# A Mamba-2 scan with an ELU feed-forward behind it: blocks of two batches by turns, and the scan's products of two blocks in one go

## The chip, the cores and the metric

The kernel runs on one core of one Trainium2 chip. The metric is the device time of one execution in microseconds (us). The kernel before takes 390.7 us (median of its runs). Kernels are compared only within the same rounds.

## The reference

The first half is a chunked Mamba-2 scan for 4 batches, 8 heads, 768 tokens, head size 32 and state size 16. The second half is a feed-forward on all 3072 tokens (256 to 2048 to 256) with an ELU between. Everything is float32; the two weights come in as float64.

```python
for c in range(nc):                                   # chunks along the sequence
    cum = np.cumsum(log_a[:, :, sl], axis=-1)
    L = np.exp(cum[:, :, :, None] - cum[:, :, None, :]) * causal
    M = np.einsum('bhin,bhjn->bhij', Cc, Bc) * L      # "scores", then weighed
    y_intra = np.einsum('bhij,bhjd->bhid', M, xc)     # "inside"
    y_inter = np.einsum('bhin,bhnd->bhid', Cc, state) * np.exp(cum)[..., None]   # "across"
    y[:, :, sl] = y_intra + y_inter
    state = decay_full * state + sum_j(Bx)            # "sums", "states"
# bridge: (B,H,S,D) -> (B*S, H*D)
h = x @ w_in
g = np.where(h > 0.0, h, np.exp(np.minimum(h, 0.0)) - 1.0)
return g @ w_out
```

The output of a chunk needs the state that the chunk before it left, so blocks of one batch form a chain. Blocks of different batches do not depend on each other.

## The kernel before: the parts that matter here

The tokens are cut into 12 blocks of 256 (3 per batch). TensorE does the feed-forward of block n-2 (second product, `l2`) and of block n (first product, `l1`) by turns in steps of 8 passes, and between these steps it visits the scan of the next blocks. A visit consists of many small products on parts of the array. A float32 product shows in the trace as two passes (MATMUL records), each with a load of its weights (one more record; the trace of before has 3546 of each); counts of the scan's small products below are counts of such passes.

```python
def sums(n, pool=p_a, tag="a"):          # one block; 24 or 32 of its small products
    ...
            nc.tensor.matmul(
                out=ps[v][32 * q:32 * q + 32, u],
                lhsT=s["sc"][toks, u, 2 * q:2 * q + 2].rearrange("p h n -> p (h n)"),
                rhs=s["x"][toks, u, 2 * D * q:2 * D * (q + 1)], start=True, stop=True,
                tile_position=(Q * v, 32 * q), skip_group_check=True)

def meet(n):                             # one visit of one block
    across(n)
    inside(n)
    if n + 1 < NP:
        sums(n + 1)
        states(n + 1)

for n in range(2, NP):
    for i in range(8):
        l2(n - 2, i)                     # second product of block n-2, step i
        if todo < len(pieces):
            w_take(todo, nc.vector)      # ScalarE's Abs of a weight piece, ...
        l1(n, i)                         # first product of block n, step i
        if todo < len(pieces):
            w_give(todo)                 # ... VectorE and GpSimd finish the piece
            w_load(todo + 6)
            todo += 1
        while lag:
            elu()
        if i == 0:                       # transfers of the next blocks
            if n + 2 < NP:
                load_bc(n + 2)
                spread_cum(n + 2)        # the decay matrix L, right after B and C
                load_x(n + 2)
            if n + 3 < NP:
                spread_exp(n + 3)
        ...                              # (cut: block 3's own steps)
        if n + 2 < NP:
            if i == 1:
                scaled(n + 2, nc.gpsimd)
            if i == 3:
                turn(n + 2)
                turn_exp(n + 2)
            if 2 <= i < 6:
                decay(n + 2, i - 2)      # ScalarE's exponentials of L
        ...
        if i == 6 and n + 1 < NP:
            meet(n + 1)
        if i == 7 and n + 2 < NP:
            scores(n + 2)
            for q in range(4):
                weigh(n + 2, q)
```

The order of these lines is also the order in which each engine gets its instructions: in the profile after the change, ScalarE begins nothing of what stands behind one waiting instruction for 15.6 us. The float64 weights are turned into float32 on the chip while the first blocks run: `todo` counts the 16 pieces, and pieces 10 to 15 are still being made when n = 2 (one in each of its steps 0 to 5).

## Time and profile before

| | before |
|---|---|
| median of 6 runs in the first comparison | 390.7 us (390.14 to 393.05) |
| span of the profiled run, mean granted clock | 388.0 us, 1.000 |
| TensorE busy | 98% of the span |
| cost of one scan visit with its sums | 1.66 to 1.75 us |
| cost of one scores visit | 0.82 us |

The last two rows come from the starts of single products: the time from the feed-forward group in front of a visit to the end of the group behind it, less 16 feed-forward passes at 0.2157 us. The busy shares and the way a block's scan sits between the feed-forward groups are shown in the prediction. The line below gives the chain of waits that ended last, as shares of the span by engine.

```profile
PE 83%; ACT 5%; DMA 3%; SPq 3%; DVE 3%; issue 1%; POOL 0%; DVEq 0%; ACTq 0%; POOLq 0%
```

"issue" is time in which an engine waited for nothing that the profile shows. Here it is 1%.

### The profile page before, as it was taken

Reading aid. Unit: us, or ns where it says so; the run is one execution under the profiler, and the core shown is the slowest. Engines: PE = TensorE matmul, PEld = TensorE weight load, DVE = VectorE, ACT = ScalarE, POOL = GpSimd, SP = SyncE. Lnnn points to the kernel's source line nnn. Section 1 sums busy time; section 2 is a strip of 40 time slices with the busy share of each in tenths; the row PEclk is TensorE's granted clock in tenths of the full one; section 3 lists DMA queues with packets and bytes.
Section 4 is the critical chain, followed back from the end, with each engine's and each line's share of the span. In section 5 each row is a group of like instructions: output and inputs, shape, how many; then the busy total and the mean of one; then the engine's idle time right before and its main releaser. Section 6 shows DMA issues by size and latency. Waiting matters only on the chain.

```text
span 388.0 us, 8744 instructions
## 1 busy us (share of the span) xinstructions
PE 381.7 (98%) x3546; PEld 323.8 (83%) x3546; DVE 136.8 (35%) x280; ACT 200.1 (52%) x480; POOL 73.0 (19%) x133
## 2 busy tenths in 40 slices
PE   8999999999999999999999999999999999999996
PEld 4678788888888888888888888888888888888885
DVE  4877867943323232323123233223232321221000
ACT  3969879662653563563554464455366234334000
POOL 6525426540120120011021012012012000000000
DMA  8979966016007007006105303402500000000000
GB/s 165 225 165 256 280 157 119 7 37 113 4 12 133 7 3 137 14 2 123 28 0 88 65 0 53 101 0 45 95 2 29 2 0 11 20 2 27 0 29 27
DMA packets 86921, 25.02 MB, mean 64 GB/s; under 512 B 77184, under 2 KB 81504, under 8 KB 86880
## 3 DMA queue, kind: packets, MB, share of 16 engines
q1 hardware_dynamic: 84704, 24.26, 29.7%
q8 instruction: 28, 0.46, 0.5%
q10 hardware_dynamic: 2176, 0.20, 0.4%
q14 instruction: 13, 0.11, 0.1%
HBM read 21.10 MB, written 3.34 MB: 63 GB/s over the span
## 4 chain that ended last, share of the span: by engine, by line
PE 83%; ACT 5%; DMA 3%; SPq 3%; DVE 3%; issue 1%; POOL 0%; DVEq 0%; ACTq 0%; POOLq 0%
PE ps_o L552 38%; PE ps_h L525 36%; PE ps_o L567 4%; PE ps_y L497 2%; ACT L L393 2%; SPq L107 2%; PE ps_g L412 1%; DMA w<-in_moe_w_in_dram 1%; PE ps_y L482 1%; DMA xr<-in_x_dram 1%; ACT e L537 1%; DMA flat<-F 1%; PE ps_st L438 1%; ACT mag L152 1%; SPq L115 1%
## 5 line engine op out<-in xcount | busy, mean ns | idle before, releaser
L525 PE MATMUL ps_h<-yT,w_in 128*128 128x256 f32 x768 | 181.3, 380 | 1.1 <-DVE g L539 0.5
L552 PE MATMUL ps_o<-w_out,g 128*128 128x256 f32 x704 | 167.3, 382 | 0.1
L525 PEld LDWEIGHTS ps_h<-yT,w_in 128*128 128x128 f32 x768 | 145.5, 190 | 22.0 <-ACT yT L508 0.9
L552 PEld LDWEIGHTS ps_o<-w_out,g 128*128 128x128 f32 x704 | 131.7, 190 | 19.5 <-issue 1.4
L539 DVE SCALAR_TENSOR_TENSOR g<-e,ps_h 128x512 f32<-128x512 f32 x96 | 65.9, 687 | 209.7 <-ACT e L538 209.6
L537 ACT ACTIVATE e<-ps_h 128x512 f32<-128x512 f32 x96 | 57.1, 595 | 137.2 <-PE ps_h L525 137.0
L538 ACT ACTIVATE e<-e 128x512 f32<-128x512 f32 x96 | 60.5, 630 | 3.0
L398 POOL TENSOR_SCALAR_AFFINE_SELECT L<-L 64x512 f32<-64x512 f32 x40 | 26.6, 665 | 132.4 <-ACT L L393 131.2
L393 ACT ACTIVATE L<-L,ncum 128x64 f32<-128x64 f32 x160 | 41.9, 334 | 0.0
L508 ACT COPY yT<-ps_y 64x128 f32<-64x128 f32 (+1 forms) x70 | 17.9, 260 | 6.7 <-PE ps_y L497 5.7
L459 POOL TENSOR_TENSOR Sx<-S_new,hmask 128x64 f32<-128x64 f32 x44 | 13.3, 304 | 20.8 <-DVE S_new L454 14.1
L421 DVE TENSOR_TENSOR M<-ps_g,L 128x256 f32<-128x256 f32 x48 | 17.1, 416 | 0.1
L558 ACT COPY ob<-ps_o 128x512 f32<-128x512 f32 x11 | 6.4, 585 | 18.4 <-PE ps_o L552 18.4
L321 POOL TENSOR_TENSOR sc<-bc,eb 128x256 f32<-128x256 f32 x12 | 7.8, 656 | 38.9 <-DMA bc<-in_B_dram 37.2
L567 PE MATMUL ps_o<-w_out,g 128*128 128x256 f32 x64 | 14.0, 379 | 0.0
L567 PEld LDWEIGHTS ps_o<-w_out,g 128*128 128x128 f32 x64 | 12.2, 190 | 1.6
L194 POOL TENSOR_TENSOR w_out<-mag,w_out 128x512 uint32<-128x512 uint32 x8 | 10.2, 1274 | 16.5 <-DVE mag L184 16.5
L194 POOL TENSOR_TENSOR w_in<-mag,w_in 128x512 uint32<-128x512 uint32 x8 | 10.2, 1277 | 15.2 <-DVE mag L184 15.2
L184 DVE SCALAR_TENSOR_TENSOR mag<-mag,sgn 128x512 uint32<-128x512 uint32 x16 | 12.3, 772 | 0.5
L454 DVE SCALAR_TENSOR_TENSOR S_new<-S_new,ec,ps_st 128x64 f32<-128x64 f32 x40 | 11.2, 279 | 2.5
L152 ACT ACTIVATE mag<-w 128x512 f32<-128x512 f32 x16 | 10.7, 671 | 1.5 <-DMA w<-in_moe_w_in_dram 1.3
L497 PE MATMUL ps_y<-M,xr 64*32 64x64 f32 x768 | 10.6, 225 | 0.0
(67 smaller groups left out, 137.5 us busy)
## 6 DMA issues: line engine op xcount, KB each, us to landing
L<-flat SPq DMA_DIRECT2D x20, 256.0 KB, 4.5
w<-in_moe_w_in_dram SPq DMA_DIRECT2D x8, 512.0 KB, 5.0
w<-in_moe_w_out_dram SPq DMA_DIRECT2D x8, 512.0 KB, 6.4
xr<-in_x_dram SPq DMA_DIRECT2D x24, 128.0 KB, 4.4
out_dram<-ob SPq DMA_DIRECT2D x11, 256.0 KB, 2.2
bc<-in_B_dram SPq DMA_DIRECT2D x24, 64.0 KB, 3.2
bc<-in_C_dram SPq DMA_DIRECT2D x22, 64.0 KB, 3.4
ec<-flat_exp SPq DMA_DIRECT2D x64, 16.0 KB, 1.8
```

What stands on the lines that cost most here:

```text
L194: nc.gpsimd.tensor_tensor(out=w, in0=w_mag[i][:, :, cols], in1=w, op=ALU.add)
L393: nc.scalar.activation(L[:, h, u], L[:, h, u], ACT.Exp, bias=ncum[:, u, row:row + 1])
L398: nc.gpsimd.affine_select(out=part, in_=part, pattern=[[0, 4], [0, 2], [1, Q]], compare_op=ALU.is_ge, fill=0.0, base=0, channel_multiplier=-1)
L421: nc.vector.tensor_tensor(out=M, in0=s["g"][q], in1=s["L"][:, 2 * q:2 * q + 2].rearrange("p k u i -> p u k i"), op=ALU.mult)
L497: nc.tensor.matmul(out=s["y"][t][v][col:col + D, u], lhsT=s["x"][toks, u, D * h:D * (h + 1)], rhs=s["M"][h // 2][toks, u, h % 2], start=Fa ...
L508: nc.scalar.copy(out=yT[n][at:at + count, t, :, Q * v:Q * v + Q], in_=s["y"][t][v][src:src + count])
L525: nc.tensor.matmul(out=ps[:, j], lhsT=w_in[:, k, m * P:(m + 1) * P], rhs=yT[n][:, k].rearrange("p u i -> p (u i)"), start=(k == 0), stop=( ...
L537: nc.scalar.activation(e, ps, ACT.Relu, scale=-1.0)
L538: nc.scalar.activation(e, e, ACT.Exp, scale=-1.0)
L539: nc.vector.scalar_tensor_tensor(out=g_of[n][:, 2 * i:2 * i + 2], in0=e, scalar=1.0, in1=ps, op0=ALU.subtract, op1=ALU.max)
L552: nc.tensor.matmul(out=o_of[n][:, ts], lhsT=g_of[n][:, m, ts * P:(ts + 1) * P], rhs=w_out[:, m], start=(m == 0 and ts == 0), stop=(m == MC ...
L567: nc.tensor.matmul(out=ps, lhsT=g_of[n][:, m, ts * P:(ts + 1) * P], rhs=w_out[:, m], start=(m == 0), stop=(m == MC - 1))
```

## The change

The intent is to save changes of tile shape on TensorE (0.145 to 0.198 us each in the trace of before, against 0.018 between two groups of the same shape). If the blocks of two batches come by turns (batch 0, batch 1, batch 0, ...), blocks 2k and 2k+1 do not depend on each other, and their scores, across, inside and sums can be done in one visit. From block 4 on there are then four visits of each kind instead of eight. The transfers of both blocks of a pair are issued in one round, in a new order. Block 3's exponentials are brought by eight small transfers instead of one product.

```diff
+    def place(n):
+        return 2 * (n // (2 * NG)) + n % 2, n // 2 % NG
 ...
-    def scores(n):                    # likewise sums, across, inside
-        gs = [psum([P, 2, 2, Q], "ps_g") for _ in range(4)]
+    def scores(*ns):
+        gs = [psum([P, len(ns), 2, 2, Q], "ps_g") for _ in range(4)]
+        for at, n in enumerate(ns):
 ...
+    def meet(*ns):
+        inside(across(*ns), *ns)
+        then = ns[-1] + 1, ns[-1] + 2
+        if then[0] < NP:
+            sums(*then)
+            for n in then:
+                states(n)
 ... in the start:
             spread_cum(3)
             load_x(3)
+            spread_exp(3)             # was first_exp(3), a product on TensorE
 ... in the main loop:
-            if i == 0:
-                if n + 2 < NP:
-                    load_bc(n + 2)
-                    spread_cum(n + 2)
-                    load_x(n + 2)
-                if n + 3 < NP:
-                    spread_exp(n + 3)
+            late = 2 if n == 2 else 3
+            m = n + late
+            if m % 2 == 0 and 4 <= m < NP:
+                if i in (0, 1):
+                    load_bc(m + i)
+                    load_x(m + i)
+                    spread_exp(m + i)
+                if i in (2, 3):
+                    spread_cum(m + i - 2)
+                if i in (4, 5):
+                    scaled(m + i - 4, nc.gpsimd)
+            m = n + 2 - n % 2
+            if 4 <= m < NP:
+                if n % 2 == 0:
+                    ...
+                    if i >= 2:
+                        decay(m + i // 6, (i - 2) % 4)
+                else:
+                    ...
+                    if i == 3:
+                        scores(m, m + 1)
+                        for q in range(4):
+                            weigh(m, q)
+                            weigh(m + 1, q)
+                    if i == 6:
+                        meet(m, m + 1)
 ... (cut: rows_of and the outputs by place(n), buffer counts, one copy on GpSimd)
```

More of the change, by code (lines that the diff above doesn't have):

```diff
@@ L70 @@
     const = ctx.enter_context(tc.tile_pool(name="const", bufs=1))
-    raw = ctx.enter_context(tc.tile_pool(name="raw", bufs=4))
+    raw = ctx.enter_context(tc.tile_pool(name="raw", bufs=3))
     att = ctx.enter_context(tc.tile_pool(name="att", bufs=2))
@@ L95 @@
     st = {}
+    def place(n):
+        return 2 * (n // (2 * NG)) + n % 2, n // 2 % NG
     def rows_of(n):
-        b, g = divmod(n, NG)
+        b, g = place(n)
         return slice(BH * g + NH * b, BH * g + NH * (b + 1))
     def load_bc(n, c_queue=nc.sync):
-        b, g = divmod(n, NG)
+        b, g = place(n)
         st.setdefault(n, {})["bc"] = raw.tile([P, 2, 2, NH, N], F32, tag="bc", name="bc")
@@ L110, in load_x @@
     def load_x(n):
-        b, g = divmod(n, NG)
-        st[n]["x"] = raw.tile([P, 2, NH * D], F32, tag="xr", name="xr")
+        b, g = place(n)
+        st[n]["x"] = raw.tile([P, 2, NH * D], F32, tag="xr", name="xr", bufs=4)
         for u in range(2):
@@ L150, in w_abs @@
     def w_abs(i):
-        w_mag[i] = conv.tile([P, 2, CW], U32, tag="mag", name="mag", bufs=3)
+        w_mag[i] = conv.tile([P, 2, CW], U32, tag="mag", name="mag")
         nc.scalar.activation(w_mag[i].bitcast(F32), w_words(i)[1].bitcast(F32), ACT.Abs)
@@ L198 @@
     w_load(0)
-    idle = const.tile([P, 4, P], BF16, name="idle")
+    idle = att.tile([P, 4, P], BF16, tag="M", name="idle", bufs=8)
     nc.vector.memset(idle, 0.0)
@@ L242 @@
         out=minus, in0=ident, scalar1=-1.0, scalar2=None, op0=ALU.mult)
-    heads = [const.tile([ROWS, NH, N], F32, name=f"heads{n}") for n in range(4)]
-    for n in range(4):
+    heads = [const.tile([ROWS, NH, N], F32, name=f"heads{n}") for n in range(3)]
+    for n in range(3):
         nc.gpsimd.tensor_copy(
@@ L400, in decay @@
                     compare_op=ALU.is_ge, fill=0.0, base=0, channel_multiplier=-1)
-    def scores(n):
-        s = st[n]
-        s["g"] = gs = [psum([P, 2, 2, Q], "ps_g") for _ in range(4)]
-        for u in range(2):
-            for v in range(2):
-                for q in range(4):
-                    rows, toks = slice(32 * q, 32 * q + 32), slice(Q * v, Q * v + Q)
-                    nc.tensor.matmul(
-                        out=gs[q][toks, u], lhsT=s["bt"][rows, u, toks],
-                        rhs=s["ctm"][rows, u, :, toks], start=True, stop=True,
-                        tile_position=(32 * q, Q * v), skip_group_check=True)
-        s["M"] = []
+    def scores(*ns):
+        gs = [psum([P, len(ns), 2, 2, Q], "ps_g") for _ in range(4)]
+        for at, n in enumerate(ns):
+            s = st[n]
+            for u in range(2):
+                for v in range(2):
+                    for q in range(4):
+                        rows, toks = slice(32 * q, 32 * q + 32), slice(Q * v, Q * v + Q)
+                        nc.tensor.matmul(
+                            out=gs[q][toks, at, u], lhsT=s["bt"][rows, u, toks],
+                            rhs=s["ctm"][rows, u, :, toks], start=True, stop=True,
+                            tile_position=(32 * q, Q * v), skip_group_check=True)
+            s["g"], s["M"] = [g[:, at] for g in gs], []
     def weigh(n, q):
@@ L426, in chunks, with sums @@
     def chunks(n):
-        return [(u, v) for u in range(2) for v in range(2) if n % NG < NG - 1 or u + v < 2]
-    def sums(n, pool=p_a, tag="a"):
-        s = st[n]
-        s["st"] = ps = [psum([P, 2, 2 * D], "ps_st"),
-                        pool.tile([P, 2, 2 * D], F32, tag=tag, name="ps_st")]
-        for u, v in chunks(n):
-            toks = slice(Q * v, Q * v + Q)
-            for q in range(4):
-                nc.tensor.matmul(
-                    out=ps[v][32 * q:32 * q + 32, u],
-                    lhsT=s["sc"][toks, u, 2 * q:2 * q + 2].rearrange("p h n -> p (h n)"),
-                    rhs=s["x"][toks, u, 2 * D * q:2 * D * (q + 1)], start=True, stop=True,
-                    tile_position=(Q * v, 32 * q), skip_group_check=True)
+        return [(u, v) for u in range(2) for v in range(2)
+                if place(n)[1] < NG - 1 or u + v < 2]
+    def sums(*ns, pool=p_a, tag="a"):
+        ps = [psum([P, len(ns), 2, 2 * D], "ps_st"),
+              pool.tile([P, len(ns), 2, 2 * D], F32, tag=tag, name="ps_st")]
+        for at, n in enumerate(ns):
+            s = st[n]
+            for u, v in chunks(n):
+                toks = slice(Q * v, Q * v + Q)
+                for q in range(4):
+                    nc.tensor.matmul(
+                        out=ps[v][32 * q:32 * q + 32, at, u],
+                        lhsT=s["sc"][toks, u, 2 * q:2 * q + 2].rearrange("p h n -> p (h n)"),
+                        rhs=s["x"][toks, u, 2 * D * q:2 * D * (q + 1)], start=True, stop=True,
+                        tile_position=(Q * v, 32 * q), skip_group_check=True)
+            s["st"] = [p[:, at] for p in ps]
     def states(n):
-        b, g = divmod(n, NG)
+        b, g = place(n)
         s = st[n]
@@ L456, in states @@
                     in1=add, op0=ALU.mult, op1=ALU.add)
-            Sx = att.tile([P, 2, D], F32, tag="Sx", name="Sx", bufs=8)
+            Sx = att.tile([P, 2, D], F32, tag="Sx", name="Sx", bufs=12)
             nc.gpsimd.tensor_tensor(
@@ L462, in states, with across @@
             at = 2 * u + v + 1
-            starts[n + at // 4, at % 4 // 2, at % 2] = Sx
+            starts[n + at // 4 * 2, at % 4 // 2, at % 2] = Sx
     def shift(n, v):
         return 2 * D * v if n else 0
-    def across(n):
-        s = st[n]
-        s["y"] = y = [[psum([P, 2, Q], "ps_y") for _ in range(2)] for _ in range(2)]
+    def across(*ns):
+        y = [[psum([P, len(ns), 2, Q], "ps_y") for _ in range(2)] for _ in range(2)]
         for u in (1, 0):
-            for v in range(2):
-                Sx = starts.pop((n, u, v), None)
-                if Sx is None:
-                    continue
-                for q in range(4):
-                    rows, col = slice(32 * q, 32 * q + 32), (64 * q + shift(n, v)) % P
-                    nc.tensor.matmul(
-                        out=y[q // 2][v][col:col + 64, u],
-                        lhsT=Sx[rows].rearrange("p k d -> p (k d)"),
-                        rhs=s["cts"][rows, u, Q * v:Q * v + Q], start=(u == 1), stop=False,
-                        tile_position=(32 * q, col), skip_group_check=True)
@@ L488, in inside @@
-    def inside(n, ts=(0, 1)):
-        s = st[n]
-        for t in ts:
-            for u in range(2):
+            for at, n in enumerate(ns):
                 for v in range(2):
-                    toks = slice(Q * v, Q * v + Q)
+                    Sx = starts.pop((n, u, v), None)
+                    if Sx is None:
+                        continue
                     for q in range(4):
-                        h, col = 4 * t + q, (D * q + shift(n, v)) % P
+                        rows, col = slice(32 * q, 32 * q + 32), (64 * q + shift(n, v)) % P
@@ L497, in inside @@
                         nc.tensor.matmul(
-                            out=s["y"][t][v][col:col + D, u],
-                            lhsT=s["x"][toks, u, D * h:D * (h + 1)],
-                            rhs=s["M"][h // 2][toks, u, h % 2], start=False, stop=True,
-                            tile_position=(Q * v, col), skip_group_check=True)
-            if t == 0:
-                yT[n] = ffn.tile([P, KC, 2, P], F32, tag="yT", name="yT")
+                            out=y[q // 2][v][col:col + 64, at, u],
@@ new lines, in across, with inside @@
+                            lhsT=Sx[rows].rearrange("p k d -> p (k d)"),
+                            rhs=st[n]["cts"][rows, u, Q * v:Q * v + Q],
+                            start=(u == 1 and at == 0), stop=False,
+                            tile_position=(32 * q, col), skip_group_check=True)
+        return y
+    def inside(y, *ns):
+        for t in range(2):
+            for at, n in enumerate(ns):
+                s = st[n]
+                for u in range(2):
+                    for v in range(2):
+                        toks = slice(Q * v, Q * v + Q)
+                        for q in range(4):
+                            h, col = 4 * t + q, (D * q + shift(n, v)) % P
+                            nc.tensor.matmul(
+                                out=y[t][v][col:col + D, at, u],
+                                lhsT=s["x"][toks, u, D * h:D * (h + 1)],
+                                rhs=s["M"][h // 2][toks, u, h % 2], start=False, stop=True,
+                                tile_position=(Q * v, col), skip_group_check=True)
+            n = ns[0]
+            if n // 2 not in yT:
+                yT[n // 2] = ffn.tile([P, KC, 2, 2, P], F32, tag="yT", name="yT")
+            out = yT[n // 2][:, t, n % 2:n % 2 + len(ns)]
@@ L508, in inside @@
                     nc.scalar.copy(
-                        out=yT[n][at:at + count, t, :, Q * v:Q * v + Q],
-                        in_=s["y"][t][v][src:src + count])
-        if 1 in ts:
+                        out=out[at:at + count, :, :, Q * v:Q * v + Q],
+                        in_=y[t][v][src:src + count])
+        for n in ns:
             st.pop(n)
@@ L526, in l1 @@
                     out=ps[:, j], lhsT=w_in[:, k, m * P:(m + 1) * P],
-                    rhs=yT[n][:, k].rearrange("p u i -> p (u i)"),
+                    rhs=yT[n // 2][:, k, n % 2].rearrange("p u i -> p (u i)"),
                     start=(k == 0), stop=(k == KC - 1))
@@ L541, in elu, with row_of @@
             op0=ALU.subtract, op1=ALU.max)
+    def row_of(n):
+        b, g = place(n)
+        return b * S + g * BLK
     o_of = {}
@@ L558, in l2 @@
             nc.scalar.copy(out=ob, in_=o_of.pop(n))
+            r0 = row_of(n)
             nc.sync.dma_start(
-                out=out[n * BLK:(n + 1) * BLK, :].rearrange("(t p) e -> p t e", p=P), in_=ob)
+                out=out[r0:r0 + BLK, :].rearrange("(t p) e -> p t e", p=P), in_=ob)
     def l2_last(n):
@@ L571, in l2_last @@
             nc.scalar.copy(out=ob[:, ts], in_=ps)
-            r0 = n * BLK + ts * P
+            r0 = row_of(n) + ts * P
             nc.sync.dma_start(out=out[r0:r0 + P, :], in_=ob[:, ts])
-    def meet(n):
-        across(n)
-        inside(n)
-        if n + 1 < NP:
-            sums(n + 1)
-            states(n + 1)
+    def meet(*ns):
[5 more added lines that the diff above has]
+                states(n)
     def w_take(i, low):
@@ L619 @@
     turn_exp(0)
-    sums(0, p_o, "o")
+    sums(0, pool=p_o, tag="o")
     first_minus(*first)
@@ L634 @@
         weigh(0, q)
-    nc.gpsimd.tensor_copy(F[3 * BH:4 * BH, 0], F[BH:2 * BH, 0])
-    second = (1, 0, 1), (1, 1, 3)
+    second = (1, 0, 0), (1, 1, 3)
     first_low(1, 0)
@@ L641 @@
     w_low(1, nc.scalar)
-    across(0)
-    inside(0)
+    inside(across(0), 0)
     w_sign(1)
@@ L672 @@
     scores(1)
-    sums(1, p_o, "o")
+    sums(1, pool=p_o, tag="o")
     weigh(1, 0)
@@ L681 @@
     w_take(4, nc.vector)
-    across(1)
-    inside(1)
+    inside(across(1), 1)
     ncum = turned(F[0:ROWS, 0], "ncum", -1.0, nc.vector)
@@ L714 @@
             load_x(3)
+            spread_exp(3)
             weigh(2, 2)
             weigh(2, 3)
-            sums(2, p_o, "o")
+            sums(2, pool=p_o, tag="o")
             states(2)
         if s == 10:
-            across(2)
-            inside(2)
+            inside(across(2), 2)
         if len(lag) > 1:
             elu()
-    spread_exp(4)
     for n in range(2, NP):
@@ L751 @@
                     turn(3)
-                    first_exp(3)
                     turn_exp(3)
@@ L757 @@
                         weigh(3, q)
-            if n + 2 < NP:
-                if i == 1:
-                    scaled(n + 2, nc.gpsimd)
-                if i == 3:
-                    turn(n + 2)
-                    turn_exp(n + 2)
-                if 2 <= i < 6:
-                    decay(n + 2, i - 2)
-            if i == 4 and n == 2:
-                sums(3)
-                states(3)
-            if i == 6 and n + 1 < NP:
-                meet(n + 1)
-            if i == 7 and n + 2 < NP:
-                scores(n + 2)
-                for q in range(4):
-                    weigh(n + 2, q)
+                if i == 4:
+                    sums(3)
+                    states(3)
+            late = 2 if n == 2 else 3
[12 more added lines that the diff above has]
+                if n % 2 == 0:
+                    if i in (5, 7):
+                        turn(m + i // 7)
+                        turn_exp(m + i // 7)
+                    if i >= 2:
+                        decay(m + i // 6, (i - 2) % 4)
+                else:
+                    if i < 2:
+                        decay(m + 1, i + 2)
+                    if i == 3:
+                        scores(m, m + 1)
+                        for q in range(4):
+                            weigh(m, q)
+                            weigh(m + 1, q)
+                    if i == 6:
+                        meet(m, m + 1)
+            if n == 2 and i == 6:
+                meet(3)
     for i in range(8):
```

## The prediction

The sum came to -3.4 for the visits, -0.43 for first_exp, +12.3 for TensorE's wait and +2.2 for half clock behind that wait: +10.7, hence 401.5. Nothing in the trace of before gives the 2.2; without it the sum is +8.5, or 399.3. The same holds for the clock term of 2 in rival (b). The pace of 0.43 under "What would show it" is seen in the trace of before at its start alone, where the seven first idle products of 512 columns stand 0.427 us apart and three later ones 0.215; that a wait brings it back is not shown there. The landing at 80.0 is 76.0 plus an estimate of 4.0, within the 3.4 to 9.8 us (median 4.5) that transfers of L took before. For "mostly idle" in rival (a): the mean busy share of the DMA engines is 0.19 from 100 us on.

> **What bounds the kernel now.** I read the page's busy shares and its costliest groups first, then TensorE's timeline over one block, then the queues of ScalarE and of the DMA issuer where the changed kernel issues in another order. Times are microseconds in the profiled run (span 388.0; the timed median is 390.8).
>
> ```profile
> PE 381.7 (98%) x3546; PEld 323.8 (83%) x3546; DVE 136.8 (35%) x280; ACT 200.1 (52%) x480; POOL 73.0 (19%) x133
> ...
> L525 PE MATMUL ps_h<-yT,w_in 128*128 128x256 f32 x768 | 181.3, 380 | 1.1 <-DVE g L539 0.5
> L552 PE MATMUL ps_o<-w_out,g 128*128 128x256 f32 x704 | 167.3, 382 | 0.1
> ```
>
> TensorE is busy 98% of the span, and 181.3 + 167.3 are the two feed-forward products (with the last block's, 14.0 more), which the change leaves alone. Only the remaining 25 us or so, the scan's small products and the start, can shrink. So I look at how one block's scan sits between them (start, length, engine, line):
>
> ```profile
> 78.61 1.89 PE L525 MATMUL ps_h<-yT,w_in 128*128 128x256 f32 x8
> 80.43 0.49 PE L482 MATMUL ps_y<-cts,Sx 32*64 32x64 f32 x24
> 80.85 0.88 PE L497 MATMUL ps_y<-M,xr 64*32 64x64 f32 x64
> 81.53 0.52 PE L438 MATMUL ps_st<-xr,sc 64*32 64x64 f32 x32
> 81.98 1.99 PE L552 MATMUL ps_o<-w_out,g 128*128 128x256 f32 x8
> 83.81 1.89 PE L525 MATMUL ps_h<-yT,w_in 128*128 128x256 f32 x8
> 85.63 0.69 PE L412 MATMUL ps_g<-ctm,bt 32*64 32x128 f32 x32
> 86.25 1.99 PE L552 MATMUL ps_o<-w_out,g 128*128 128x256 f32 x8
> 88.08 1.89 PE L525 MATMUL ps_h<-yT,w_in 128*128 128x256 f32 x8
> ```
>
> Subtract starts. An undisturbed feed-forward group of eight takes 1.73 (91.54 to 93.26 in the same view). After 78.61 the scan starts at +1.82, so entering costs 0.09; the feed-forward group after a scan takes 83.81 - 81.98 = 1.83, so leaving costs another 0.10. The single instructions of the trace say where the rest sits: from the last L482 to the first L497 it is 0.146, from the last L438 to the first L552 0.145, from the last L412 to the first L552 0.198, but from L497 to L438, which have the same tile shape (64*32), only 0.018. So a change of tile shape costs about 0.1 to 0.2, and the pitch within a shape is 7 to 13 ns per instruction.
>
> [...]
>
> **The change part by part.**
>
> (1) Fewer visits to the scan. Before, blocks 3 to 11 each have one visit for across/inside/sums and blocks 4 to 11 one for scores. After, block 3 has its own, and the pairs (4,5), (6,7), (8,9), (10,11) have one of each: four visits of each kind fewer. The products themselves stay. A visit's fixed part: across/inside/sums 0.09 in + 0.146 + 0.145 + 0.10 out = 0.48; scores 0.09 + 0.18 + 0.10 = 0.37. Saved: 4 x 0.85 = 3.4, all on TensorE, which sets the end.
>
> (2) The product that spreads block 3's exponentials (first_exp) goes; on TensorE that is 60.46 to 60.89: 0.43 saved. Eight small transfers take its place.
>
> (3) GpSimd loses a copy of F (0.48) and one of four head copies (0.4), ScalarE merges 128-wide yT copies into 256-wide ones. Neither is on the path: GpSimd is 19% busy, ScalarE 52%. I count 0.
>
> (4) **Transfers are issued in another order**, and this costs. Before, block 4's decay matrix L comes right after its B and C:
>
> ```profile
> 46.87 6.16 SPq L138 DMA_DIRECT2D w<-in_moe_w_out_dram  x1
> 53.07 4.46 SPq L304 DMA_DIRECT2D ec<-flat_exp  x8
> 57.64 0.39 SPq L107 DMA_DIRECT2D bc<-in_B_dram  x1
> ...
> 60.06 1.68 SPq L295 DMA_DIRECT2D L<-flat  x2
> 61.85 1.17 SPq L115 DMA_DIRECT2D xr<-in_x_dram  x2
> 63.46 5.00 SPq L304 DMA_DIRECT2D ec<-flat_exp  x8
> ```
>
> and ScalarE uses it at once, in its program after the elu of block 2, step 2:
>
> ```profile
> 64.56 0.59 ACT L537 ACTIVATE e<-ps_h 128x512 f32<-128x512 f32 x1
> 65.18 0.63 ACT L538 ACTIVATE e<-e 128x512 f32<-128x512 f32 x1
> 65.71 1.05 ACT L393 ACTIVATE L<-L,ncum 128x64 f32<-128x64 f32 x4
> 66.67 0.67 ACT L152 ACTIVATE mag<-w 128x512 f32<-128x512 f32 x1
> ```
>
> In the built changed kernel that decay stands at the same place in ScalarE's order, but the issuer's order is ec(3) x8, last weight piece, then bc x4, x x2, ec x8 for block 4, the same 14 for block 5, and only then L(4). I assume the issuer comes free at 53.1 as before ([...]the profile shows 6.16 for one issue). Then: ec(3) 4.4, weight 0.6 gives 58.1; per block 2.4 + 1.2 + 4.7 = 8.3, twice 16.6, plus holds (the first ec at 63.46 took 1.66 instead of 0.42; bigger ones come later in the trace), say 1.3 in all, gives 76.0. L(4) is two issues; the page gives a median of 4.5 from issue to landing[...]. **L(4) lands at about 80.0 instead of before 65.7.**
>
> ScalarE then stands from about 65.8 to 80. Behind the decay in its queue is the Abs of weight piece 13, which the second product needs at step 5. TensorE goes on as long as its operands are there: without first_exp, and with the transpose of block 4 moved behind step 5, it reaches that product at 72.99 - 0.43 - 0.44 = 72.1. The piece is ready after the decay 0.96, Abs 0.67, two VectorE steps 0.42 + 0.69, GpSimd's sum 1.28 and some 0.4 of handing on: 4.4 after landing, 84.4. TensorE idles 84.4 - 72.1 = 12.3.[...] ScalarE and VectorE then catch up[...]; pieces 14 and 15 come 2.7 apart and the steps are 3.45 apart, so I see no second stall. The later pairs load a whole round earlier (issued in round 3 for use in round 4), with some 10 us of slack.
>
> Sum: -3.4 - 0.43 + 12.3 + 2.2 = +10.7, so 390.8 + 10.7 = **401.5**.
>
> **Rivals.**
> (a) The transfers land in time and only (1) and (2) act: 390.8 - 3.9 = 386.9, within 2%. For it: DMA is mostly idle after 100 us and the byte count is the same. Against it: 36 issues stand between the first ec(3) and L(4), and even at the bare 0.46 to 0.5 each that is 17 us after 53.1, or 70 plus the landing.
> (b) The wait is there but shorter: the issuer isn't held to 53.1 because a small ec stands there instead of a 512 KB piece, and no hold comes later. L(4) at 75.5, idle about 8, clock 2: 397, within 2%. Against it: later first ecs were held as well.
> (c) The paired visits make PSUM or ScalarE the bound: [...]the yT copies are twice as wide, with seven buffers in rotation. ScalarE has some 14 of 30.6 us idle per block, so at most a few tenths per pair: +1.
> (d) Weight transfer and block 4's loads fight for bandwidth and L(4) lands at 83: 404 to 405.
>
> **Range and chances.** The landing time is the weak term: 76 to 84 moves the result from 397.5 to 405.5. The saving is good to about 0.7, the clock term to 1. Eight in ten: 396 to 406. The 2% line is at 398.6, 2.9 below my value; the range implies a standard deviation of about 3.9, so the line is 0.75 of it away: slower 0.75, within 2% 0.23 (mostly b, a little a), faster 0.02.
>
> **What would show it.** In the changed profile: one ScalarE wait of 12 to 16 us before L of the decay line, released by the L transfer, near 66 to 80; one TensorE wait of about 12 at the second product, released by GpSimd's w_out sum, soon after 72; the feed-forward products after it 0.43 apart instead of 0.216 for a few us; from block 4 on, pairs of blocks taking about 61.25 - 0.85 = 60.4 instead of 61.25. The prediction is wrong if L(4) is issued before 70, if ScalarE doesn't wait there, or if waits of over 1 us appear on TensorE in the later pairs.

## The result and the profile after

The changed kernel takes 414.06 us (median of 6, 411.64 to 414.31) against 390.7. The ratio is 1.0566, with a 95% interval of 1.0525 to 1.0607: slower. A ratio here is the mean time of one kernel's fast runs over that of the other's of the same rounds, so it is not quite the ratio of the medians. The direction was predicted; the size, 401.5 with a range up to 406, was not.

From the page of the changed kernel: the granted clock in 40 slices (tenths), the queue of TensorE's instructions (packets, MB, share), the chain that ended last, and two groups (busy time, mean ns, idle time before them and what ended it).

```profile
PEclk9999999669999999999999999899999999999999
...
q8 instruction: 28, 0.46, 0.5%
...
PE 83%; issue 7%; ACT 4%; DMA 2%; DVE 2%; SPq 1%; POOL 1%; DVEq 0%; ACTq 0%; POOLq 0%
...
L569 PE MATMUL ps_o<-w_out,g 128*128 128x256 f32 x704 | 169.8, 386 | 13.2 <-POOL w_out L198 13.2
...
L397 ACT ACTIVATE L<-L,ncum 128x64 f32<-128x64 f32 x160 | 41.9, 334 | 15.6 <-DMA L<-flat 15.6
```

The last two lines are the wait that the prediction described: ScalarE waits 15.6 us for the transfer of L, and TensorE's second product waits 13.2 us for GpSimd's sum of a weight piece (before: 0.1). The clock falls in slices 8 and 9, and once more in a slice much later: its record says 0.500 from 75.76 to 89.41 and from 256.67 to 260.08, and 1.000 between. The share "issue" in the chain has grown from 1% to 7%. Of this, the list of the chain's pieces puts 16.1 us in front of GpSimd's sum of the weight piece, which is the first loss seen from GpSimd; four more pieces of 1.7 to 2.1 us lie at 129, 191, 254 and 318 us, in the scan's visits, and do not belong to it.

**The first loss, as predicted.** The DMA issuer's timeline (start, length, line, transfer):

```profile
47.17 9.77 SPq L308 DMA_DIRECT2D ec<-flat_exp  x8
...
62.89 4.38 SPq L308 DMA_DIRECT2D ec<-flat_exp  x8
...
71.66 4.89 SPq L308 DMA_DIRECT2D ec<-flat_exp  x8
76.60 2.37 SPq L299 DMA_DIRECT2D L<-flat  x4
```

The eight small transfers of block 3 hold the issuer from 47.17 to 57. Those of blocks 4 and 5 follow, and L(4) is issued only at 76.60. ScalarE's timeline and then TensorE's over the same time:

```profile
64.89 0.63 ACT L551 ACTIVATE e<-e 128x512 f32<-128x512 f32 x1
81.16 1.06 ACT L397 ACTIVATE L<-L,ncum 128x64 f32<-128x64 f32 x4 [15.64 <-DMA L<-flat]
```

```profile
71.70 0.45 PE L445 MATMUL ps_st<-xr,sc 64*32 64x64 f32 x32
85.36 3.78 PE L569 MATMUL ps_o<-w_out,g 128*128 128x256 f32 x8 [13.21 <-POOL w_out L198]
88.94 2.13 PE L538 MATMUL ps_h<-yT,w_in 128*128 128x256 f32 x8
```

L(4) is there at 81.16, and TensorE stands 13.2 us. The group behind the wait takes 88.94 - 85.36 = 3.58 instead of 1.73: half clock (passes 0.427 apart instead of 0.216), about 2.0 us with the start of the next group.

**The second loss, not predicted.** TensorE's timeline over the first paired visit (blocks 4 and 5):

```profile
126.32 0.99 PE L490 MATMUL ps_y<-cts,Sx 32*64 32x64 f32 x64
127.24 1.51 PE L508 MATMUL ps_y<-M,xr 64*32 64x64 f32 x128
128.55 0.78 PE L445 MATMUL ps_st<-xr,sc 64*32 64x64 f32 x56
131.11 0.32 PE L445 MATMUL ps_st<-xr,sc 64*32 64x64 f32 x8 [1.78 <-issue]
```

In the middle of the sums, 56 products in, TensorE stops for 1.8 us and waits for nothing that has a semaphore. From start to start it is 1.99 us (129.12 to 131.11). All four paired visits have such a gap: 1.99, 1.95, 2.27 and 1.88 us, two in the sums and two among the products of inside. After the third, one feed-forward group takes 3.47 instead of 1.83: half clock once more (passes 0.427 apart), about 1.6 us:

```profile
256.49 0.30 PE L445 MATMUL ps_st<-xr,sc 64*32 64x64 f32 x3 [2.06 <-issue]
256.72 3.64 PE L569 MATMUL ps_o<-w_out,g 128*128 128x256 f32 x8
260.19 1.89 PE L538 MATMUL ps_h<-yT,w_in 128*128 128x256 f32 x8
```

The places of the gaps are the clue. I sorted all 7,172 records of TensorE (products, weight loads, semaphores) by start and counted. The first records after the gaps are numbers 3009, 4033, 5313 and 6337, counted from 0. Less 193, these are 11, 15, 20 and 24 times 256, exactly. The instruction queue on the page has 28 packets of 0.46 MB in all, which is 16.4 KB each, and 7,172 / 28 = 256. So every gap lies where one packet of instructions ends and the next begins. The transfers of these packets fit too (28 fetches and 28 borders, matched by order). At 127.78 TensorE enters the packet before the gap, the fetch that goes with this border by order is recorded at 128.77, and the first instruction of the following packet starts at 131.11, while the packet in hand was used up at 129.12. In the four visits a packet was used up in 1.33 to 1.46 us, and the next came 3.33, 3.41, 3.60 and 3.34 us after the entry. In plain feed-forward a packet lasts 27 us (27.4 for each of the two that end at 372 and 399 us).

**The account.** Profiled spans: 409.8 - 388.0 = +21.8. Wait for the weight piece 13.2; half clock after it 2.0; four gaps 8.0 (8.09 less the normal pitches); half clock after the third 1.6; saved visits -2.3 (visit by visit as in the table above, without gap and slow clock; block 3's visit, which now holds the sums of two blocks, is counted in); product of first_exp -0.4. The sum is 22.1.

### The profile page after: what moved, and what is told of

Same layout as the page of the kernel before. It is cut to its first block, busy times and chain, and to the rows that moved or that the text cites. A ratio compares the mean times of both kernels' runs of the same rounds, so it can differ in the third digit from the quotient of the medians.

```text
span 409.8 us, 8664 instructions
## 1 busy us (share of the span) xinstructions
PE 382.7 (93%) x3544; PEld 326.9 (80%) x3544; DVE 138.1 (34%) x280; ACT 196.6 (48%) x455; POOL 72.5 (18%) x131
## 3 DMA queue, kind: packets, MB, share of 16 engines
HBM read 21.23 MB, written 3.34 MB: 60 GB/s over the span
## 4 chain that ended last, share of the span: by engine, by line
PE 83%; issue 7%; ACT 4%; DMA 2%; DVE 2%; SPq 1%; POOL 1%; DVEq 0%; ACTq 0%; POOLq 0%
PE ps_o L569 37%; PE ps_h L538 36%; PE ps_o L585 3%; PE ps_y L508 2%; PE ps_y L490 1%; PE ps_g L417 1%; DMA w<-in_moe_w_in_dram 1%; ACT L L397 1%; DMA bc<-in_C_dram 1%; PE ps_st L445 1%; ACT e L550 1%; POOL w_out L198 1%; ACT mag L156 1%; PE ps_tc L335 0%; PE ps_tb L335 0%
## 5 line engine op out<-in xcount | busy, mean ns | idle before, releaser
L569 PE MATMUL ps_o<-w_out,g 128*128 128x256 f32 x704 | 169.8, 386 | 13.2 <-POOL w_out L198 13.2
L569 PEld LDWEIGHTS ps_o<-w_out,g 128*128 128x128 f32 x704 | 134.3, 193 | 32.6 <-POOL w_out L198 13.4
L397 ACT ACTIVATE L<-L,ncum 128x64 f32<-128x64 f32 x160 | 41.9, 334 | 15.6 <-DMA L<-flat 15.6
L467 POOL TENSOR_TENSOR Sx<-S_new,hmask 128x64 f32<-128x64 f32 x44 | 13.2, 305 | 59.8 <-DVE S_new L462 40.4
L521 ACT COPY yT<-ps_y 64x256 f32<-64x256 f32 (+3 forms) x46 | 14.3, 319 | 10.0 <-PE ps_y L508 9.6
L585 PE MATMUL ps_o<-w_out,g 128*128 128x256 f32 x64 | 14.0, 379 | 0.0
L585 PEld LDWEIGHTS ps_o<-w_out,g 128*128 128x128 f32 x64 | 12.2, 190 | 1.7
L198 POOL TENSOR_TENSOR w_in<-mag,w_in 128x512 uint32<-128x512 uint32 x8 | 10.4, 1295 | 15.6 <-DVE mag L188 15.6
L181 DVE TENSOR_SCALAR mag<-mag 128x512 f32<-128x512 f32 x16 | 7.8, 486 | 14.8 <-ACT mag L156 14.8
L508 PEld LDWEIGHTS ps_y<-M,xr 64*32 64x32 f32 x768 | 8.4, 105 | 4.2 <-issue 3.7
```

Source lines behind the costliest of these rows:

```text
L198: nc.gpsimd.tensor_tensor(out=w, in0=w_mag[i][:, :, cols], in1=w, op=ALU.add)
L397: nc.scalar.activation(L[:, h, u], L[:, h, u], ACT.Exp, bias=ncum[:, u, row:row + 1])
L508: nc.tensor.matmul(out=y[t][v][col:col + D, at, u], lhsT=s["x"][toks, u, D * h:D * (h + 1)], rhs=s["M"][h // 2][toks, u, h % 2], start=Fal ...
L521: nc.scalar.copy(out=out[at:at + count, :, :, Q * v:Q * v + Q], in_=y[t][v][src:src + count])
L569: nc.tensor.matmul(out=o_of[n][:, ts], lhsT=g_of[n][:, m, ts * P:(ts + 1) * P], rhs=w_out[:, m], start=(m == 0 and ts == 0), stop=(m == MC ...
L585: nc.tensor.matmul(out=ps, lhsT=g_of[n][:, m, ts * P:(ts + 1) * P], rhs=w_out[:, m], start=(m == 0), stop=(m == MC - 1))
```

## The experiments

Theory: two independent losses, the late L(4) (with the half clock behind it) and gaps in the supply of instructions inside the paired visits. Rivals: the paired visit loses through PSUM banks, ScalarE or its mere length; or the new block order costs something everywhere.

### e1_order: the old order of transfers, everything else as changed

```diff
                 if i in (0, 1):
                     load_bc(m + i)
+                    spread_cum(m + i)
                     load_x(m + i)
                     spread_exp(m + i)
-                if i in (2, 3):
-                    spread_cum(m + i - 2)
```

> Undoes one part of the change: each block's L transfer is issued right after its B and C again, the paired products stay. Theory (the change loses time in two places: 13.2 us of waiting for L(4) plus 2.0 us at half clock after it, and four gaps of about 2.0 us in the paired visits): the 15.2 us go and the gaps stay, about 414.1 - 15.2 = 399 us. Rival (nearly all of the loss comes from the transfers, the gaps in the pairs are an after-effect of the late start): about 387 to 391 us, no gaps.

Measured: 399.32 us (median of 4; one of them, 403.21, is left out), ratio 1.0179 [1.0113, 1.0245], so against the 2% line it is unclear. ScalarE's wait for L fell from 15.6 to 1.4:

```profile
67.25 1.06 ACT L397 ACTIVATE L<-L,ncum 128x64 f32<-128x64 f32 x4 [1.43 <-DMA L<-flat]
```

TensorE had no wait at the second product any more. The four gaps stayed, at the same four records (3009, 4033, 5313, 6337), with 2.24, 1.98, 2.02 and 1.73 us; half clock followed the first and the third. So the order of transfers accounts for about 15 us, and the gaps do not come from it. The first gap of e1_order:

```profile
113.65 0.78 PE L445 MATMUL ps_st<-xr,sc 64*32 64x64 f32 x56
116.45 0.32 PE L445 MATMUL ps_st<-xr,sc 64*32 64x64 f32 x8 [2.02 <-issue]
```

### e2_split: late transfers kept, the paired visit cut in three

```diff
-                    if i == 6:
-                        meet(m, m + 1)
+                    if i in (5, 6):
+                        inside(across(m + i - 5), m + i - 5)
+                    if i == 7 and m + 2 < NP:
+                        sums(m + 2, m + 3)
+                        states(m + 2)
+                        states(m + 3)
```

> The changed kernel with its late transfers, but each pair's visit of 224 to 256 small products split into three (block m, block m+1, sums of the next pair), with feed-forward groups between. Theory (TensorE outruns its instruction fetch, 256 instructions per 16 KB block[...]): no gap over 1 us inside any visit; minus 4 x 2.0, minus 1.7 to 3.5 of half clock after gaps, plus 4 x 0.82 for the extra visits: 405.5 to 408 us. Rival (the gap is a wait for data of the paired block, PSUM or states): gaps of about 2 us stay somewhere in the visits and the time stays 412 to 415 us or grows.

Measured: 406.04 us (405.72 to 407.43), ratio 1.038 [1.0331, 1.0428]. The wait at the second product is still there (14.1 us in this profile), and no visit of blocks 4 to 11 has a gap of over 0.35 us. Two of the three short visits:

```profile
126.46 0.89 PE L508 MATMUL ps_y<-M,xr 64*32 64x64 f32 x64
...
135.81 0.86 PE L445 MATMUL ps_st<-xr,sc 64*32 64x64 f32 x64
```

The same products run without the "issue" in brackets. The theory's range held.

### e3_both: both of these

> Both parts together: transfers in the old order and split visits. Theory: both losses go; what is left of the change is the missing product for block 3 (0.43 us) and scores in pairs, paid back by the separate visit for sums: 389.5 to 391 us, like the kernel before. If the losses are not additive (one hidden behind the other), e1 and e2 together would explain more or less than the 23.4 us between the kernels.

Measured: 390.5 us (390.42 to 390.69), ratio 0.9977 [0.9933, 1.002], clock 1.000 in every run. Both losses are gone together. The new block order itself costs nothing that these runs could show. Cut in three, the pairs also save next to nothing: the visits of blocks 4 to 11 cost 19.6 us, those of the kernel before 20.0, but block 3's visit, with the sums of two blocks in it, costs 2.08 instead of 1.75.

### e4_phase: the kernel before, with 32 more instructions at the start

If instruction supply is the cause, the kernel before should show it too once a visit coincides with a packet.

```diff
-    idle_products(7)
+    idle_products(5)
+    for _ in range(18):
+        nc.tensor.matmul(
+            out=ps_idle[:, 0, 0:8], lhsT=idle[:, 0], rhs=idle[:, 0, 0:8], start=True, stop=True)
```

> The kernel before, with 32 more TensorE instructions at its very start (18 tiny idle products for 2 of the 7 large ones), so that the visit of block 4 at about 141.6 us, 256 instructions long, starts where a 256-instruction block starts. No data, buffer or wait is touched. Instruction-fetch theory: one new gap of 1.5 to 2 us at the end of that visit, none in the other visits; +1.6 us, or +3.3 if the clock drops after it. Rival (gap from data or buffers of the pairs): no gap, 390.7 us.

Measured: 391.63 us (390.71 to 392.86), ratio 1.0012 [0.9954, 1.0069]. The aim was met: a packet began with the first record of the visit (142.99; it is block 5's, which the text above calls block 4's) and was used up at 144.39. The gap did not come:

```profile
144.09 0.52 PE L441 MATMUL ps_st<-xr,sc 64*32 64x64 f32 x32
144.54 1.78 PE L555 MATMUL ps_o<-w_out,g 128*128 128x256 f32 x7
```

So the simple form of the theory, that a packet used up in under 3 us always stalls, is wrong. The trace suggests why: the fetch that goes by order with the border at 142.99 is recorded at 140.04, 3 us ahead of the visit. In feed-forward stretches of all these traces, past the start, the fetch that belongs to a border (matched by order, one for each border) mostly comes 2.5 to 4.5 us ahead of the border (2.16 to 4.46 in the changed kernel past 100 us); for borders well inside a visit it mostly comes 0.5 to 1.2 us after it (0.57 to 1.03 there, and 1.05 to 1.55 for the borders at the gaps). What sets this lead, and why there is none inside a burst of small products, no run shows. The refined theory is that only a packet which is both entered and used up well inside one visit costs 2 us. A visit of 256 instructions cannot hold one, whereas visits of 386 to 514, as the pairs have, can. One gap did come with the new phase, where none was expected: 0.76 us among the products of block 0's inside, at 14.65 and record 449 = 193 + 256. The kernel before has none in that visit.

### e5_shift224 and e6_shift80: e1_order with the packet borders moved

Nothing but a number of tiny products is put into the start, so the visits are the same and only the borders move in them.

```diff
+    for _ in range(56):               # 20 in e6_shift80; four instructions each
+        nc.tensor.matmul(
+            out=none[0:64, 0, 0:8], lhsT=ident[0:32, 0:64], rhs=ident[0:32, 0:8],
+            start=True, stop=True, tile_position=(0, 0), skip_group_check=True)
     inside(across(0), 0)
```

> The changed kernel with the old order of transfers (as in e1_order) and 56 tiny products (224 TensorE instructions) put before block 0's across, with no other change: all paired visits stay whole. TensorE's records are counted in time order; in e1_order the four gaps lie at borders of 256 instructions, 498, 343, 476 and 353 instructions into the four paired visits. e4_phase, where a visit of 256 instructions filled one whole instruction block in 1.40 us without a gap, refutes the simple form of the theory (a block used up in under 3 us always stalls); the refined form is that [...]a gap comes only when a whole block is entered well inside a visit and used up inside it. Refined theory, by visit: borders move to 18/274/530 in the first, 119/375 in the second, -4/252/508 in the third, 129/385 in the fourth. So the gaps of the first (2.2) and third (2.0) fall to under 0.4, that of the second stays about 2.0 (now 119+256=375 instructions in), that of the fourth falls to about 1.6 (the visit ends there). Time 399.3 - 4.2 - 0.3 + 0.6 for the tiny products = about 395.5. Rival (the paired visits themselves are too long for PSUM, a queue of TensorE or ScalarE, not instruction supply): four gaps of about 2 us at the same places in the visits, 399 to 400.

> As e5_shift224 but with 20 tiny products (80 instructions). Refined theory of instruction supply: borders move to 162/418 in the first visit, 7/263/519 in the second, 140/396 in the third, 17/273 in the fourth. So now the second and fourth gaps go (under 0.4 each) and the first and third stay at about 2 us, at 418 and 396 instructions into the visit: the pattern of e5_shift224 turned round. Time 399.3 - 2.0 - 1.7 + 0.2 = about 395.8. Rival (the visit's length itself, or the PSUM or ScalarE): four gaps, 399 to 400. If gaps were tied to certain visits (first and third alike in both kernels), both are wrong.

Measured gaps in the four paired visits, start to start, in us:

| kernel | blocks 4, 5 | 6, 7 | 8, 9 | 10, 11 |
|---|---|---|---|---|
| e1_order | 2.24 | 1.98 | 2.02 | 1.73 |
| e5_shift224 | 0.59 | 1.99 | 0.52 | 1.81 |
| e6_shift80 | 1.82 | 0.69 | 1.80 | 0.80 |

The first two visits of e5_shift224, and of e6_shift80, at their gap:

```profile
123.31 0.78 PE L508 MATMUL ps_y<-M,xr 64*32 64x64 f32 x55 [0.38 <-issue]
...
186.85 0.76 PE L445 MATMUL ps_st<-xr,sc 64*32 64x64 f32 x53 [1.77 <-issue]
```

```profile
120.18 0.71 PE L445 MATMUL ps_st<-xr,sc 64*32 64x64 f32 x47 [1.60 <-issue]
...
180.80 0.69 PE L508 MATMUL ps_y<-M,xr 64*32 64x64 f32 x44 [0.48 <-issue]
```

The pattern turns round as foretold. In e5_shift224 the second visit's gap moved from inside's products into the sums, where its border had moved. All gaps again lie at records 193 plus a multiple of 256. PSUM, ScalarE and the length of the visit are the same in the three kernels, so this decides for the supply of instructions. Two details missed. Where a border lies at the very start of a visit, 0.5 to 0.8 us stay, not under 0.4 (why stays open). And e5_shift224 took 402.57 us (401.94 to 402.63), ratio 1.03 [1.0272, 1.0327], not 395.5: its tiny products took 8.5 us instead of the 0.6 that I had assumed. Their 112 passes of 8 columns stand 58 ns apart at first and 107 ns from 15.15 on; the scan's passes of 64 columns stand 10 to 14 ns apart, and why these are so much slower was not shown. At 15.15, 4.3 us after the first of them and with no pause in between, the granted clock fell to half, and it stayed so to 25.39, through the next feed-forward group (3.75 us busy). e6_shift80, with few of them, took 396.89 (395.5 to 398.61), ratio 1.0146 [1.0109, 1.0184], against an expected 395.8.

### e7_sums and e9_phase_free: can the pairs be made to pay?

e7_sums takes the old order of transfers, moves a pair's sums into its own scores visit, so that visits have at most 386 instructions, and sets the phase with 18 tiny products.

```diff
                     if i == 3:
                         scores(m, m + 1)
+                        sums(m, m + 1)
                         ...
+                        states(m)
+                        states(m + 1)
 ... and meet() without its sums and states
```

> Candidate to beat both: old order of transfers, scores and across/inside still paired, but a pair's sums move from the end of the pair's across/inside visit before it into its own scores visit, and 18 tiny products (72 instructions) set the phase. Visits are then at most 386 (across/inside) and 256 (scores/sums) instructions, and the borders fall at 170, 15/271, 148, 25/281 in the four and at 142, -13/243, 120, -3/253 in the scores visits, so that no block after an in-visit entry is used up inside a visit. Theory: no gap over 0.5 us in any visit; saving 3.9 of the predicted terms less 4 x 0.15 for one more change of tile shape per pair less 0.2 for the tiny products, 390.6 - 3.1 = about 387.5, ratio 0.992. Rival (length of the visits themselves): gaps of 1 to 2 us stay in the visits of 386 instructions, 392 to 396.

Measured: 392.22 us (391.29 to 393.8), ratio 1.0042 [1.0016, 1.0069]; the expected 387.5 was missed. The first and third pair have no gap, the second and fourth 0.78 and 0.81, with borders 13 and 19 records into the visit; one of 0.62 lies in the start, at 55.90 and record 1473 = 193 + 5 x 256. The tiny products again cost more than thought:

```profile
11.65 2.49 PE L655 MATMUL ps_none<-ident 32*64 32x8 f32 x35
...
179.24 0.67 PE L508 MATMUL ps_y<-M,xr 64*32 64x64 f32 x42 [0.56 <-issue]
```

e9_phase_free sets nearly the same phase by cutting the idle products of the start in four instead.

```diff
-            nc.tensor.matmul(out=ps_idle, lhsT=idle[:, 0], rhs=idle, start=True, stop=True)
+            for k in range(4):
+                nc.tensor.matmul(
+                    out=ps_idle[:, k], lhsT=idle[:, 0], rhs=idle[:, k], start=True, stop=True)
 ...
-    idle_products(7)
+    idle_products(8)
```

> As e7_sums (old order of transfers, pairs kept, sums in the scores visit), but the phase is set without the 18 tiny products: in e7_sums they took 2.5 us by themselves[...] and left a half clock of about 1.9 us behind them. Instead the idle products of the start are cut in four (11 x 4 products of 128 columns instead of 10 of 512), 68 more instructions at about the same time. Borders: 174, 17/273, 148, 23/279 in the four across/inside visits. In e7_sums a border 13 or 19 instructions into the visit still gave a gap of 0.8, so two gaps of 0.8 to 1.0 stay, in the second and fourth. Theory: 392.2 - 3.6 = 388.6, between 388 and 389.5, ratio 0.994 to 0.997. Rival (e7_sums lost its time elsewhere, such as in PSUM banks held by the sums): 391 to 392.

Measured: 391.24 us (390.85 to 392.96), ratio 1.0007 [0.9983, 1.0031]; the expected 388.6 was missed. The number is the rival's, but the trace does not put the loss in the sums. The later visits behave as expected (gaps of 0.79 and 0.46), and one gap of 0.59 stands at record 1473, much as in e7_sums, but a new gap appeared early, in block 1's visit, at record 961 = 193 + 3 x 256:

```profile
27.30 0.83 PE L510 MATMUL ps_y<-M,xr 64*32 64x64 f32 x58
29.84 0.31 PE L510 MATMUL ps_y<-M,xr 64*32 64x64 f32 x6 [1.71 <-issue]
```

It took 1.92 us from start to start, with half clock behind it (passes 0.425 apart from 31.16 to 33.71). This packet had lasted 4.16 us (23.75 to 27.91), longer than those that stalled later (1.33 to 1.46 in the changed kernel). But the fetch that goes with its entry by order is recorded only at 27.41, 3.7 us after it, where the packets that stalled in the changed kernel's late visits show 0.8 to 1.0. The DMA engines are 60 to 90% busy in these slices of the page and mostly under 20% past 100 us; whether this held the fetch back was not shown. The phase that helps the late visits hurts in the start. No version that I ran beats the kernel before by more than the noise; e3_both and e9_phase_free equal it.

These gap-free visits also allow the saving itself to be measured. The pair's scan visit without sums costs 2.56 us in e7_sums, and the single one 1.43 in e3_both: 2 x 1.43 - 2.56 = 0.30 saved. The scores visit costs 1.34 for a pair and 0.82 for one: 2 x 0.82 - 1.34 = 0.30 saved.

### e8_warm: the changed kernel with TensorE kept busy through its wait

```diff
+            if (n, i) == (2, 5):
+                warm = psum([P, 4, 60], "ps_warm")
+                for _ in range(128):      # 256 instructions: the phase stays
+                    nc.tensor.matmul(
+                        out=warm, lhsT=ident16,
+                        rhs=low16[:, 0:60].unsqueeze(1).to_broadcast([P, 4, 60]),
+                        start=True, stop=True, skip_group_check=True)
             l2(n - 2, i)
```

> The changed kernel as it is (late transfers, whole pairs), with 128 idle products of 240 columns (256 instructions, so that the phase of the instruction blocks stays) just before the product that stands 13.2 us waiting for the weight piece: TensorE works through the wait. Theory that the half clock after the wait is a cost of its own of about 2 us (group of eight 3.57 instead of 1.73): the group after the wait takes 1.8, and the time falls by about 2.0 to 412, the wait for the weight piece ending at the same 85.4 and the four gaps of 2 us staying. Rival (the slow groups come from something else, such as traffic in the weight piece's DMA or slow operands): the groups after 85.4 stay at about 3.6 and the time stays at 414.

Measured: 412.44 us (410.99 to 413.74), ratio 1.0557 [1.0527, 1.0587]. In the profile the half clock after the wait is gone:

```profile
72.98 13.29 PE L745 MATMUL ps_warm<-low,ident 128*128 128x240 bf16 x128
86.28 1.99 PE L569 MATMUL ps_o<-w_out,g 128*128 128x256 f32 x8
```

The group behind the idle products takes 1.83 (86.28 to 88.11) instead of 3.58, and this run's clock record has no half clock there, so the slow group was the clock and not its operands. The four gaps stayed (1.99, 1.94, 2.09, 2.04 us; 1.99, 1.95, 2.27, 1.88 in the changed kernel), as was expected at the same phase. The time alone does not show the saving: its interval overlaps that of the changed kernel, and in this profile half clock followed two gaps instead of one (7 to 8 passes some 0.425 us apart each time). Not every gap is followed by half clock (one of four in the changed kernel, two of four in e1_order and here), and the mean clock changes from run to run: the four runs of e1_order have mean clocks from 0.987 to 1.000, and the one at 1.000 is the fastest (396.67). I take this to be a good part of the spread of the kernels with gaps; that is argued, not shown.

## Why the prediction was wrong, point by point

- **What bounds the kernel, and part (4), the late transfers: right.** L(4) arrived at 81.2 (predicted 80.0), TensorE waited 13.2 (12.3), the half clock behind it cost 2.0 (2.2, for which the trace of before gave no ground). e1_order takes this away by restoring the order alone, and e8_warm takes the clock term away alone. Rivals (a), (b) and (d) had L(4) land in time, earlier or at 83, and fall with the landing at 81.2.
- **Part (2), the product of first_exp: as predicted.** It is no longer on TensorE. Its eight transfers hold the issuer for 9.8 us, where the prediction counted 4.4 from a later start; that the two errors nearly cancel is luck.
- **Part (1), fewer visits: the mechanism right, the term too large.** The fixed part of a visit came out as 0.30 us for each kind, not 0.48 and 0.37, so 2.4 instead of 3.4 for the four pairs. The prediction took the pitch of the products as the same in a longer visit. It is not: across takes 0.41 us for one block (126.05 to 126.46 in e2_split) and 0.92 for two (116.02 to 116.94 in e7_sums), although the pair has one change of shape less. Its pitch of 7 to 13 ns "per instruction" is also misread: passes stand 10 to 14 ns apart by their starts, and each is two instructions. No sum used it, but a packet's life in a burst hangs on it.
- **Rival (c) is the step that failed.** It asked whether paired visits could become bound by something else, looked only at PSUM and ScalarE, and gave "at most a few tenths per pair: +1". The supply of TensorE's instructions was not considered. It cost 2.0 us per pair, 8.0 in all, plus half clock after some gaps (1.6 in the profile). In terms of the account above, the predicted +10.7 became +22.1: gaps 8.0, half clock after a gap 1.6, a longer wait 0.9, less clock after it -0.2, and 1.1 that the visits did not save make up the 11.4 between. The medians lie 23.4 apart and the profiled spans 21.8; the profiled run of the changed kernel was the fastest of its six. e2_split removes this term alone, and e5_shift224 and e6_shift80 move it at will.
- **The text named the sign in time.** It said that the prediction is wrong "if waits of over 1 us appear on TensorE in the later pairs". They did.

Could it have been foreseen? The trace of before holds the numbers needed: 28 instruction packets for some 7,200 records, small products at some 6.5 ns per instruction (the visit in the prediction: 120 passes, each with its weight load, from 80.43 to 81.98), and hence, as an estimate, a packet gone in 1.7 us in a long enough burst. What it does not hold is the 3.3 to 3.6 us from entering a packet to having the next, measured at the four gaps of the changed kernel, because no visit of the kernel before is long enough to show it.

## What to carry to other kernels

When many tiny instructions are gathered into one burst, ask how fast the burst eats instructions, not only how fast the array does the products: here a burst in which TensorE entered and used up a whole packet of 256 instructions (in 1.33 to 1.46 us) stopped for 1.73 to 2.27 us (changed kernel and e1_order), while, away from the busy start, bursts up to 256 instructions did not (e4_phase; none over 0.35 us in e2_split), and two feed-forward groups (3.45 us) between two bursts, at about 0.3 us for the extra visit (e7_sums against e3_both), were enough to hide it. A gap labelled "issue" that lies at equal distances modulo 256 in the sorted records of an engine is the sign to look for, and a shift of the phase by a few dozen instructions is a cheap test. And when transfers are reordered for a later use, follow the first use after the start separately: in the changed kernel L(6) was issued at 117.33 for use at 146.64, while L(4) came 15.6 us too late.
